# Expert weights' low parts on VectorE, and a float64 decode that checks instead of zeroing and starts one expert earlier

## The chip, the cores and the metric

The kernel runs on one core of a Trainium2 chip. The metric is the device time of one execution, in microseconds (us). Engines are named as in the profile: PE (matrix engine, PEld its weight loads), DVE (vector), ACT (scalar), POOL (GpSimd) and SP (the engine that issues nearly all DMAs, in one order). The engines run side by side, each works through its own instructions strictly in order, and they wait for one another by semaphores.

## The reference

Three layers follow one another. The attention is a recurrence over 768 steps for 4 x 8 heads with a 40 x 40 state. Its output, 3072 tokens of 320 numbers, goes to a mixture of 8 experts, each token to the one with the largest logit. A dense layer follows. Cut to the parts in which the change lies:

```python
x = attn_out.transpose(0, 2, 1, 3).reshape(3072, 320)
expert_idx = argmax(x @ w_gate, axis=1)
for e in range(8):                        # w1[e]: 320x1024, w2[e]: 1024x320, float32
    xe = x[expert_idx == e]
    out[expert_idx == e] = gate * (maximum(xe @ w1[e], 0) @ w2[e])
h = out @ w_in                            # 320x2048, given in float64
g = maximum(h, 0) + alpha * minimum(h, 0)
return (g @ w_out).astype(float32)        # 2048x320, given in float64
```

## The kernel before

The program has three stretches: attention with routing, the eight experts (here expert 0 to expert 7), and the dense layer in six blocks of 512 tokens. A scheduler fixes each engine's order at build time; the program text and `issue_after` only bound it. The change lies in the experts' stretch.

**An expert.** Up to 448 tokens of one expert are computed together. Matmuls take float32 operands rounded to a high part, and a second, low part is added by more matmuls. `hidden` makes one slice of 128 hidden units: eight matmuls into `ph`, then ACT writes the high part `hh` (L1048) and DVE the low parts (L1051, once 64 columns of `hh` and once `hl`). `layer2` then multiplies `hh` and `hl` with the second weights into the sums `po`: eleven matmuls. PE takes `hidden` of slice f+1 before `layer2` of slice f, and `ph` has two buffers, so PE stops when `hh` or `hl` of a slice comes too late. Expert 0 is computed in two halves of its tokens.

**Weights of an expert** (`prep_expert`). Seven DMAs bring `w1[e]` and `w2[e]` into a ring of three buffers `raw`. ACT copies each to the high part (L985, L1001), and the engine `eng` subtracts the high part from `raw` (L987, L989, L1002): six subtractions per expert, 128x1024 twice, 64x1024, 128x960 twice, 128x640. Only then is the `raw` buffer free. For expert 0 `eng` is DVE, for experts 1 to 7 POOL. Three places hold split weights, so expert e+3 can be prepared once expert e has ended.

**The decode** (`decode`, `from_f64`). `w_in` and `w_out` are turned from float64 to float32 in 20 pieces of 128x512: SP loads a piece as pairs of 32-bit words (`r64`, two buffers, 512 KB), DVE builds the float32 bits in three operations (L214, L215, L216), ACT squares the upper words (L217, `sq`, one buffer), and a fourth DVE operation (L218) multiplies by "square at least 2^-30 in float terms", so that numbers too small for the bit trick become zero. SP writes the result (`dec`, 256 KB) to DRAM. It begins in the program text at expert 1, slice 0, after that slice's `hh` and `hl`. The dense layer's weights are read back from expert 6 on.

**A flag** collects conditions under which a general, slow version of the kernel has to run (never with these inputs); `to_flag` reduces it over the partitions with a transposition on PE, at expert 1, slice 4.

Of the kernel before, what the change touches and what calls it, by code (L numbers as in the profile page):

```python
# [8 lines left out]
F32 = mybir.dt.float32  # L9
# [3 lines left out]
U32 = mybir.dt.uint32  # L13
AF = mybir.ActivationFunctionType
ALU = mybir.AluOpType
AX = mybir.AxisListType
# [3 lines left out]
P = 128  # L20
B, H, S, D = 4, 8, 768, 40
N = B * S
DM = H * D
E = 8
F1 = 1024
F2 = 2048
# [13 lines left out]
def f32(ap):  # L40
    return ap.bitcast(F32)
# [168 lines left out]
def from_f64(nc, dst, raw, sq):  # L210

    lo, up = raw[..., 0], raw[..., 1]
    t = dst.bitcast(U32)
    nc.vector.tensor_scalar(t, up, 0x07FFFFFF, 3, op0=ALU.bitwise_and, op1=ALU.logical_shift_left)  # L214
    nc.vector.scalar_tensor_tensor(t, up, 0xC0000000, t, op0=ALU.bitwise_and, op1=ALU.bitwise_or)  # L215
    nc.vector.scalar_tensor_tensor(t, lo, 29, t, op0=ALU.logical_shift_right, op1=ALU.bitwise_or)  # L216
    nc.scalar.activation(sq, f32(up), AF.Square)  # L217
    nc.vector.scalar_tensor_tensor(dst, sq, 2.0 ** -30, dst, op0=ALU.is_ge, op1=ALU.mult)  # L218


def words(ap):
# [10 lines left out]
def whole(gen):  # L232
    for _ in gen:
        pass
# [695 lines left out]
class Moe:  # L930
# [27 lines left out]
    def decode(self, src, name):  # L958

        nc = self.nc  # L960
        n = 512
        out = self.dp.tile(list(src.shape), F32, name=name)
        flat = lambda ap: ap.rearrange("r c -> (r c)").rearrange("(p n) -> p n", p=P)
        to, wo = flat(out), words(flat(src))
        for c in range(0, to.shape[1], n):
            r64 = self.r6.tile([P, n, 2], U32, name="r64", bufs=2)
            nc.sync.dma_start(r64, wo[:, c:c + n])
            dec = self.r6.tile([P, n], F32, name="dec", bufs=2)
            sq = self.r6.tile([P, n], F32, name="sq", bufs=1)
            from_f64(nc, dec, r64, sq)  # L970
            nc.sync.dma_start(to[:, c:c + n], dec)
        return out

# [95 lines left out]
    def run(self, ctx, to_flag):  # L1069
        nc, k, tc = self.nc, self.k, self.tc  # L1070
        for i in (1, 2):
            self.wp.append(ctx.enter_context(tc.tile_pool(name=f"fm_w{i}", bufs=1, reuse_waits="tile")))
        cp = ctx.enter_context(tc.tile_pool(name="fm_c", bufs=1, reuse_waits="tile"))
# [5 lines left out]
        sums = lambda: [p.tile([P, DM], F32, name=f"po{t}") for t, p in enumerate((pa, pa, pb, pb))]  # L1079
        r6 = ExitStack()  # L1080
        self.r6 = r6.enter_context(tc.tile_pool(name="fm_r6", bufs=1, reuse_waits="tile"))
        load = self.load_x(0, EARLY)
        nxt = win = prep = w_in = w_out = None
        for e in range(E):
            w1s, w2s = self.wts[e]
            po = sums()
            ye = sp.tile([P, 4, DM], F32, name="ye", tag="orow", bufs=1)
            ys = self.rt.ys_d[e * CAP:(e + 1) * CAP, :]

            def group(xt, t0, t1, x0, tiles, ts=None, between=None):  # L1090

                ts = ts or range(t0, t1)
                n = min(t1 * P, CAP) - t0 * P
                prev = None
                for f in range(NF1):
                    hh, hl = tiles(f)
                    self.hidden(w1s, f, xt, x0, x0 + n, hh, hl)
                    if prev is not None:
                        self.layer2(po, *prev, w2s, f - 1, NF1, True, ts, t0)
                    prev = hh, hl  # L1100
                    if between:
                        between(f)
                self.layer2(po, *prev, w2s, NF1 - 1, NF1, True, ts, t0)

            def to_sbuf(t):
                if t == 3:
                    nc.scalar.copy(ye[:HT, t, :], po[t][HT:])  # L1107
                    nc.vector.tensor_tensor(ye[:HT, t, :], po[t][:HT], ye[:HT, t, :], op=ALU.add)
                else:
                    (nc.vector.tensor_copy if t % 2 else nc.scalar.copy)(ye[:, t, :], po[t])  # L1110

            def between(f):
                nonlocal nxt, win, prep, w_in, w_out
                if e == E - 2 and f == 4:
                    win = self.whole("win")
                    prep = self.prep_in(win, w_in, nc.gpsimd)
                if e == E - 2 and f >= 4:
                    for _ in range(2):
                        next(prep, None)
                if e == E - 1:  # L1120
                    with tc.issue_after(self.hh_i.ins):
                        next(prep, None)
                if f == 1 and e + 1 < E:
                    with tc.issue_after(self.rt.last.ins), tc.issue_after(self.x_dma.ins):
                        whole(self.prep_expert(e + 1, nc.gpsimd))
                if (e, f) == (1, 4):
                    to_flag(self.psum_t(P)[:1])
                if (e, f) == (1, 0):
                    with tc.issue_after(self.hh_i.ins), tc.issue_after(self.hl_i.ins):
                        w_in, w_out = self.decode(self.w_in, "w_in"), self.decode(self.w_out, "w_out")  # L1130
                if f == 4 and e + 1 < E:
                    nxt = self.load_x(e + 1)()

            ring = lambda f: [sp.tile([P, 4 * P], F32R, name=n, tag=n) for n in ("hh", "hl")]
            if e == 0:
                group(self.xt0, 0, EARLY, 0, lambda f: [self.ap.tile([P, EARLY * P], F32R, name=n, bufs=2) for n in ("ehh", "ehl")])
                xt = load()
                group(xt, EARLY, 4, 0, ring, between=between)
            elif e == E - 1:

                hs = [[hp.tile([P, 2 * P], F32R, name=f"{n}{f}") for n in ("hh", "hl")] for f in range(NF1)]
                group(xt, 0, 2, 0, lambda f: hs[f], (0,), between)
                to_sbuf(0)
                nc.sync.dma_start(ys[:P, :], ye[:, 0])
                with tc.issue_after(self.last.ins):
                    for f in range(NF1):
                        self.layer2(po, *hs[f], w2s, f, NF1, True, (1,))
                    group(xt, 2, 4, 2 * P, ring)
            else:
                group(xt, 0, 4, 0, ring, between=between)  # L1150
            for t in range(1 if e == E - 1 else 0, 4):
                to_sbuf(t)
            for rows, to in self.rows(ye, ys, 1 if e == E - 1 else 0):
                nc.sync.dma_start(to, rows)
            if e == E - 2:
                r6.close()
                hp = ctx.enter_context(tc.tile_pool(name="fm_h", bufs=1, reuse_waits="tile"))
                wout = self.whole("wout")
                prep = self.prep_out(wout, w_out, nc.gpsimd)
                win = win.rearrange("p (c f) -> p c f", c=5)  # L1160
                wout = wout.rearrange("p (s f d) -> p s f d", s=2, d=DM)
            xt = nxt
# [5 lines left out]
        for i in range(N // BT):  # L1168
            po = sums()
            prev = None  # L1170
            for f in range(NF2):
                ph = pg.tile([P, BT], F32, name="ph")
                gemm_k(nc, ph, win, f * P, (f + 1) * P, xt, 0, BT)
                g = sp.tile([P, BT], F32, name="g")
                nc.vector.tensor_scalar(g, ph, 0.0, al[:, f:f + 1], op0=ALU.min, op1=ALU.mult)  # L1175
                nc.vector.scalar_tensor_tensor(g, ph, 0.0, g, op0=ALU.max, op1=ALU.add)  # L1176
                hh = sp.tile([P, BT], F32R, name="gh", tag="hh")
                hl = sp.tile([P, BT], F32R, name="gl", tag="hl")
                lo = split(nc, hh, hl, g, nc.gpsimd)
                if prev is not None:  # L1180
                    self.layer2(po, *prev, wout, f - 1, NF2, False)
                prev = (hh, hl)
                if f == 8 and i + 1 < N // BT:
                    with tc.issue_after(lo.ins):
                        nxt = self.load_x2(i + 1, E * CAP)
# [14 lines left out]
def the_kernel(tc, r, kk, v, w, a, b, wP, kbP, aP, rvP, vrow, w_gate, w1, w2, w_in, w_out, alpha, out):  # L1200
    nc = tc.nc
    with ExitStack() as ctx:
# [6 lines left out]
        k.upper = cp.tile([P, P], BF16, name="upper")  # L1209
        k.iota8 = cp.tile([P, E], F32, name="iota8")  # L1210
        okm = cp.tile([P, 1], F32, name="okm")
        flag = cp.tile([1, 3], F32, name="flag")
        flag_i = cp.tile([1, 1], I32, name="flag_i")

        def to_flag(pk):

            nc.tensor.transpose(pk, okm, k.ident)
            nc.vector.tensor_reduce(flag[:, 0:1], pk, axis=AX.X, op=ALU.min)
            nc.vector.tensor_scalar(flag[:, 0:1], flag[:, 0:1], 0.5, None, op0=ALU.is_lt)
            nc.vector.tensor_reduce(flag[:, 2:3], flag[:, 0:2], axis=AX.X, op=ALU.max)  # L1220
            nc.vector.tensor_copy(flag_i, flag[:, 2:3])
# [62 lines left out]
```

## Time and profile before

| | |
|---|---|
| median of 3 runs | 1208.76 us (1205.51, 1208.76, 1222.03) |
| the profiled execution's own time | 1201.46 us |
| its span in the trace | 1199.7 us |
| busy: PE, DVE, ACT, POOL | 89%, 63%, 47%, 46% of the span |
| experts 0 to 7 in the trace | 570.5 to 842 us |
| dense layer | 842 us to the end |

PE is busy for most of the span, but the share is an average over stretches. A waiting engine does not show in it, and neither does PE's clock, which stands beside it as a share of full speed. A row of a group names the line of the kernel, the engine, the operation and "output <- input"; queue rows (SPq) are DMA issues.

### The profile page before, as it was taken

Reading aid. Unit: us, or ns where it says so; the run is one execution under the profiler, and the core shown is the slowest. Engines: PE = TensorE matmul, PEld = TensorE weight load, DVE = VectorE, ACT = ScalarE, POOL = GpSimd, SP = SyncE. Lnnn points to the kernel's source line nnn. Section 1 sums busy time; section 2 is a strip of 40 time slices with the busy share of each in tenths; the row PEclk is TensorE's granted clock in tenths of the full one; section 3 lists DMA queues with packets and bytes.
Section 4 is the critical chain, followed back from the end, with each engine's and each line's share of the span. In section 5 each row is a group of like instructions: output and inputs, shape, how many; then the busy total and the mean of one; then the engine's idle time right before and its main releaser. Section 6 shows DMA issues by size and latency. Waiting matters only on the chain.

```text
span 1199.7 us, 24756 instructions
## 1 busy us (share of the span) xinstructions
PE 1064.8 (89%) x9565; PEld 945.1 (79%) x9565; DVE 758.7 (63%) x1536; ACT 563.9 (47%) x1412; POOL 556.1 (46%) x498
## 2 busy tenths in 40 slices
PE   2659989988979989888897988999999999999997
PEld 2548777767868868776886877999899999999996
DVE  9896596997796987845369787333444444454542
ACT  3543568666666767887454434444121222121211
POOL 6636156467267362522574334445343435343432
PEclk7655689888789889999999898999999999999999
DMA  3531222232223211252687776442000000000100
GB/s 113 144 128 43 47 69 77 62 81 76 50 71 90 63 44 40 67 150 51 194 259 240 242 229 206 135 123 85 15 22 22 23 23 22 23 25 20 38 8 25
DMA packets 98080, 103.35 MB, mean 86 GB/s; under 512 B 58404, under 2 KB 78884, under 8 KB 97956
## 3 DMA queue, kind: packets, MB, share of 16 engines
q1 hardware_dynamic: 95652, 93.83, 27.1%
q0 software_dynamic: 2304, 7.87, 2.1%
q8 instruction: 78, 1.28, 0.4%
q14 instruction: 46, 0.38, 0.1%
HBM read 79.39 MB, written 22.28 MB: 85 GB/s over the span
## 4 chain that ended last, share of the span: by engine, by line
PE 57%; DVE 23%; issue 6%; DMA 5%; ACT 5%; POOL 3%; SPq 0%; DVEq 0%; POOLq 0%; ACTq 0%
PE ph L238 20%; PE po L238 19%; DVE tmp L506 4%; DVE ut L508 3%; PE lp L461 3%; PE pp L572 2%; PE yc L628 2%; PE yp L538 2%; PE zp L532 2%; DVE q L435 2%; PE sa L612 1%; DMA raw<-in_moe_w_dram 1%; DVE sm L632 1%; DVE dec L215 1%; PE rp L600 1%
## 5 line engine op out<-in xcount | busy, mean ns | idle before, releaser
L229 POOL TENSOR_TENSOR gl<-g,gh 128x512 fp32r<-128x512 f32 x96 | 123.9, 1293 | 211.8 <-ACT gh L228 128.1
L228 ACT ACTIVATE gh<-g 128x512 fp32r<-128x512 f32 x96 | 60.7, 632 | 249.4 <-DVE g L1176 173.9
L1175 DVE TENSOR_SCALAR g<-ph,al 128x512 f32<-128x512 f32 x96 | 72.1, 751 | 156.9 <-POOL gl L229 77.0
L238 PE MATMUL ph<-x2thi,win 128*128 128x512 f32 x480 | 157.0, 392 | 0.0
L238 PE MATMUL po<-wout,gh 128*128 128x320 f32 x768 | 139.0, 309 | 0.0
L238 PEld LDWEIGHTS po<-wout,gh 128*128 128x128 f32 x768 | 122.0, 188 | 5.4
L238 PE MATMUL ph<-x2tlo,win 128*128 128x512 f32 x288 | 113.5, 394 | 0.0
L238 PE MATMUL po<-we,hh 128*128 128x320 f32 (+1 forms) x480 | 92.3, 320 | 19.1 <-DVE hh L1051 12.4
L238 PE MATMUL ph<-xthi,we 128*128 128x448 f32 (+2 forms) x360 | 98.6, 346 | 2.7 <-ACT ye L1107 2.6
L238 PEld LDWEIGHTS ph<-x2thi,win 128*128 128x128 f32 x480 | 88.5, 188 | 13.2
L238 PEld LDWEIGHTS po<-we,hh 128*128 128x128 f32 (+1 forms) x480 | 75.6, 185 | 24.6 <-DVE hh L1051 13.8
L506 DVE TENSOR_TENSOR tmp<-ul,ut 128x31 f32<-128x31 f32 (+15 forms) x186 | 90.7, 487 | 3.3
L461 PE MATMUL lp<-kb,abd 128*128 128x128 f32 x352 | 66.2, 343 | 25.9 <-DVE la L469 12.1
L508 DVE TENSOR_TENSOR ut<-ut,tmp 128x31 f32<-128x31 f32 (+15 forms) x186 | 84.3, 453 | 3.6
L586 POOL TENSOR_SCALAR_AFFINE_SELECT va<-vg 64x512 f32<-64x512 f32 x48 | 37.2, 776 | 99.1 <-ACT vg L585 51.7
L238 PE MATMUL po<-wout,gl 128*128 128x320 f32 x384 | 82.9, 311 | 0.0
L461 PEld LDWEIGHTS lp<-kb,abd 128*128 128x128 f32 x352 | 57.5, 245 | 29.6 <-POOL abd L442 14.1
L442 POOL TENSOR_TENSOR abd<-ra,q 40x512 f32<-40x512 f32 x44 | 61.7, 1403 | 37.5 <-PE ap L485 16.8
L238 PE MATMUL ph<-xtlo,we 128*128 128x448 f32 (+2 forms) x216 | 74.7, 346 | 0.0
L238 PEld LDWEIGHTS ph<-xthi,we 128*128 128x128 f32 x360 | 67.0, 196 | 6.7 <-ACT ye L1107 2.9
L1176 DVE SCALAR_TENSOR_TENSOR g<-ph,g 128x512 f32<-128x512 f32 x96 | 66.3, 690 | 3.1
L238 PEld LDWEIGHTS po<-wout,gl 128*128 128x128 f32 x384 | 64.1, 188 | 2.8
(208 smaller groups left out, 2442.7 us busy)
## 6 DMA issues: line engine op xcount, KB each, us to landing
raw<-in_moe_w_dram SPq DMA_DIRECT2D x16, 512.0 KB
rv<-in_rvP_dram SPq DMA_DIRECT2D x48, 160.0 KB
raw<-in_moe_w_dram SPq DMA_DIRECT2D x16, 480.0 KB
kb<-in_kbP_dram SPq DMA_DIRECT2D x44, 160.0 KB
r<-in_moe_w_in_dram SPq DMA_DIRECT2D x10, 512.0 KB
r<-in_moe_w_out_dram SPq DMA_DIRECT2D x10, 512.0 KB
xs_d<-tt SPq DMA_DIRECT2D x8, 560.0 KB
raw<-in_moe_w_dram SPq DMA_DIRECT2D x16, 256.0 KB
```

The source lines that it names most:

```text
L228: nc.scalar.activation(hi, src, AF.Copy)
L229: return lo_eng.tensor_tensor(lo, src, f32(hi), op=ALU.subtract)
L238: return nc.tensor.matmul(out, lhsT=lhsT, rhs=rhs, start=start, stop=stop)
L435: nc.vector.tensor_tensor_scan(qt.rearrange("p a c t -> p (a c t)"), wz[:, :nw], self.d1q, 0.0, ALU.mult, ALU.max)
L442: nc.gpsimd.tensor_tensor(abd[r, :, q * C:(q + 1) * C], ra[r], qc[r, :, :C], op=ALU.mult)
L461: nc.tensor.matmul(lp[:, i], lhsT=abd[:, i, c2, :], rhs=kb[:, i, c2, :], start=True, stop=True)
L506: nc.vector.tensor_tensor(tv, ul[:, j, j + 1:].unsqueeze(2).to_broadcast([P, n, m]), ut[:, j, :m].unsqueeze(1).to_broadcast([P, n, m]), op ...
L508: nc.vector.tensor_tensor(ut[:, j + 1:, :m], ut[:, j + 1:, :m], tv, op=ALU.subtract)
L532: nc.tensor.matmul(zp[lo, c2, u], lhsT=l1[hi, 2 * half + c2, u, :], rhs=tt[hi, c2, u, q * 64 + 32:q * 64 + 64], start=True, stop=True)
L586: nc.gpsimd.affine_select(x.va[:C].rearrange("p a b c -> p (a b) c")[:, :, D:], x.vg[:C].rearrange("p a b c -> p (a b) c")[:, :, D:], patt ...
L1175: nc.vector.tensor_scalar(g, ph, 0.0, al[:, f:f + 1], op0=ALU.min, op1=ALU.mult)
L1176: nc.vector.scalar_tensor_tensor(g, ph, 0.0, g, op0=ALU.max, op1=ALU.add)
```

## The change

1. Experts 1 to 7: the subtractions (L987, L989, L1002) go from POOL to DVE. The dense layer's own weights stay on POOL.
2. The decode uses `from_normal_f64`: three DVE operations as before and no fourth; ACT squares and then runs a second operation, relu(1 - 2^30 x square), whose sum per partition goes into one column of `below`. A column above zero means that there was a number to be zeroed.
3. The decode begins in the program text at expert 0, slice 3 (second half), not at expert 1, slice 0.
4. `to_flag` takes the maximum of `below` into the condition and is called at the dense layer's first block, slice 4.

```diff
+def from_normal_f64(nc, dst, raw, sq, one, below):
+    lo, up = raw[..., 0], raw[..., 1]
+    t = dst.bitcast(U32)
+    nc.vector.tensor_scalar(t, up, 0x07FFFFFF, 3, op0=ALU.bitwise_and, op1=ALU.logical_shift_left)
+    nc.vector.scalar_tensor_tensor(t, up, 0xC0000000, t, op0=ALU.bitwise_and, op1=ALU.bitwise_or)
+    nc.vector.scalar_tensor_tensor(t, lo, 29, t, op0=ALU.logical_shift_right, op1=ALU.bitwise_or)
+    nc.scalar.activation(sq, f32(up), AF.Square)
+    nc.scalar.activation(sq, sq, AF.Relu, bias=one, scale=-2.0 ** 30, accum_out=below)
...
-            from_f64(nc, dec, r64, sq)
+            from_normal_f64(nc, dec, r64, sq, self.one, self.below[:, self.nb:self.nb + 1])
+            self.nb += 1
...
-                        whole(self.prep_expert(e + 1, nc.gpsimd))
-                if (e, f) == (1, 4):
-                    to_flag(self.psum_t(P)[:1])
-                if (e, f) == (1, 0):
+                        whole(self.prep_expert(e + 1, nc.vector))
+                if (e, f) == (0, 3):
                     with tc.issue_after(self.hh_i.ins), tc.issue_after(self.hl_i.ins):
                         w_in, w_out = self.decode(self.w_in, "w_in"), self.decode(self.w_out, "w_out")
...
+                if (i, f) == (0, 4):
+                    to_flag(self.psum_t(P)[:1], self.below)
...
-        def to_flag(pk):
+        def to_flag(pk, below):
+            nc.vector.tensor_reduce(low, below, axis=AX.X, op=ALU.max)
+            nc.vector.scalar_tensor_tensor(okm, low, 0.0, okm, op0=ALU.is_le, op1=ALU.mult)
```

In the changed kernel the numbers of these lines are higher: L214, L215, L216 are L225, L226, L227; L987, L989, L1002 are L999, L1001, L1014; L1051 is L1063; L967 and L971 (load and write of a piece) are L978 and L983.

DVE where expert 1 ends and expert 2 goes on: `ye` are the copies of expert 1's output, `hh` and `hl` after them belong to expert 2. Before:

```order
L1110 COPY ye<-po_7716 128x320
L1108 TENSOR_TENSOR ye<-po_7718,ye 64x320
L218 SCALAR_TENSOR_TENSOR dec<-sq,dec 128x512
L214 TENSOR_SCALAR dec<-r_7795 128x512
L215 SCALAR_TENSOR_TENSOR dec<-r_7795,dec 128x512
L216 SCALAR_TENSOR_TENSOR dec<-r_7795,dec 128x512
L1051 SCALAR_TENSOR_TENSOR hh<-ph,hh 128x64
L1051 SCALAR_TENSOR_TENSOR hl<-ph,hh 128x384
```

The same place now (`we_8497` are the weights of expert 4):

```order
L1126 COPY ye<-po_7922 128x320
L1124 TENSOR_TENSOR ye<-po_7924,ye 64x320
L227 SCALAR_TENSOR_TENSOR dec<-r_7694,dec 128x512
L999 TENSOR_TENSOR we_8497<-raw,we_8497 128x1024
L225 TENSOR_SCALAR dec<-r_7705 128x512
L999 TENSOR_TENSOR we_8497<-raw,we_8497 128x1024
L226 SCALAR_TENSOR_TENSOR dec<-r_7705,dec 128x512
L1001 TENSOR_TENSOR we_8497<-raw,we_8497 64x1024
L1063 SCALAR_TENSOR_TENSOR hh<-ph,hh 128x64
L1063 SCALAR_TENSOR_TENSOR hl<-ph,hh 128x384
```

Four decode operations stood between the outputs of expert 1 and the next `hh`; now three of the decode and three subtractions stand there. Over the experts the 20 pieces stand at 4, 5, 7 and 4 writes in experts 0, 1, 2 and 3; before they stood in experts 1 to 4.

POOL after the last routed row (the scatter into `xs_d`), before:

```order
L901 DMA xs_d<-xr,sli 3584x320 x2
L987 TENSOR_TENSOR we_7535<-raw,we_7535 128x1024 x2
L989 TENSOR_TENSOR we_7535<-raw,we_7535 64x1024
L1002 TENSOR_TENSOR we_7535<-raw,we_7535 128x960 x2
L1002 TENSOR_TENSOR we_7535<-raw,we_7535 128x640
```

And now:

```order
L912 DMA xs_d<-xr,sli 3584x320 x2
L1096 MEMSET one 128x1
L999 TENSOR_TENSOR win<-raw,win 128x1024 x2
L1001 TENSOR_TENSOR win<-raw,win 64x1024
L999 TENSOR_TENSOR win<-raw,win 128x1024 x2
```

From the end of the routing to the dense layer's weights (`win`, expert 6) POOL has no tile left to work on.

SP in expert 2, between the writes of expert 1's and expert 2's outputs, now (each written piece is followed by a load; the rows left out are the weights of expert 4):

```order
L983 DMA w_out<-dec 128x512
L978 DMA r_7745<-in_moe_w_out_dram 128x1024
L983 DMA w_out<-dec 128x512
L978 DMA r_7755<-in_moe_w_out_dram 128x1024
L983 DMA w_out<-dec 128x512
L978 DMA r_7765<-in_moe_w_out_dram 128x1024
L1027 DMA xe<-xs_d 128x3x320
L1027 DMA xe<-xs_d 64x320
L983 DMA w_out<-dec 128x512
L978 DMA r_7775<-in_moe_w_out_dram 128x1024
```

Seven pieces are loaded and seven written in this stretch, beside seven DMAs of weights; in the kernel before five were loaded and six written between these two outputs.

## Rows read from the trace of the kernel before

**Rows 1.** Stretches (experts 0-5): PE, PEld, DVE, ACT, POOL busy; clock; DMA share, GB/s.

```profile
570.50:613.00 42.50, 38.27 (x264) 35.25 (x265) 15.66 (x56) 21.88 (x43) 25.61 (x13) 0.94 0.67 203
613.00:646.50 33.50, 29.43 (x164) 26.35 (x163) 29.02 (x42) 15.93 (x27) 19.00 (x8) 0.97 0.83 261
646.50:684.80 38.30, 31.73 (x171) 28.83 (x169) 31.97 (x47) 16.23 (x28) 14.38 (x6) 0.91 0.84 259
684.80:722.40 37.60, 32.41 (x164) 28.89 (x164) 30.81 (x48) 16.40 (x28) 14.22 (x6) 0.91 0.69 221
722.40:756.20 33.80, 28.61 (x155) 26.00 (x156) 22.47 (x34) 13.85 (x24) 14.17 (x6) 0.90 0.54 162
756.20:784.10 27.90, 27.90 (x166) 26.02 (x165) 8.77 (x23) 12.66 (x22) 13.20 (x6) 1.00 0.48 144
```

**Rows 2.** Waits, 569 to 735: total us, times, longest.

```profile
ACT sq L217 <- DVE dec L218: 24.5, 8, 6.0
PE po L238 <- DVE hh L1051: 12.4, 5, 4.4
ACT we L985 <- DMA raw<-in_moe_w_dram: 11.8, 9, 3.5
ACT sq L217 <- DMA r<-in_moe_w_out_dram: 9.7, 3, 5.2
DVE dec L214 <- DMA w_out<-dec: 6.2, 3, 3.5
PE po L238 <- ACT hh L1048: 5.0, 3, 1.7
```

**Rows 3.** Instructions in time, after expert 1's end: start, us; brackets: idle before, releaser.

```profile
649.82 1.87 DVE L218 SCALAR_TENSOR_TENSOR dec<-sq,dec 128x512 f32<-128x512 f32 x1
...
650.75 0.52 ACT L1048 ACTIVATE hh<-ph 128x448 fp32r<-128x448 f32 x1
...
653.08 1.29 PE L238 MATMUL po<-we,hh 128*128 128x320 f32 x7
654.00 2.41 POOL L989 TENSOR_TENSOR we<-raw,we 64x1024 fp32r<-64x1024 f32 x1
654.24 2.72 DVE L215 SCALAR_TENSOR_TENSOR dec<-r,dec 128x512 uint32<-128x512 uint32 x1
...
657.60 0.21 DVE L1051 SCALAR_TENSOR_TENSOR hh<-ph,hh 128x64 fp32r<-128x64 f32 x1
...
657.87 0.90 PE L238 MATMUL po<-we,hh 128*128 128x320 f32 x2 [3.50 <-DVE hh L1051]
```

**Rows 4.** The decode's operations on tile dec: ns min/median/max.

```profile
L214 DVE TENSOR_SCALAR dec<-r x20: 409/423/2596, 612.1 to 735.2; 128x512 uint32<-128x512 uint32 x20
L215 DVE SCALAR_TENSOR_TENSOR dec<-r,dec x20: 676/693/2833, 614.5 to 735.7; 128x512 uint32<-128x512 uint32 x20
```

**Rows 5.** Decode's DVE instructions alone, sum over experts 0 to 6.

```profile
sum 238.80, DVE 85.00; mean DVE 12.14
```

**Rows 6.** Subtractions of weights by engine (tile raw): ns min/median/max.

```profile
L987 POOL TENSOR_TENSOR we<-raw,we x14: 2367/2404/3959, 583.0 to 760.8; 128x1024 fp32r<-128x1024 f32 x14
...
L1002 DVE TENSOR_TENSOR we<-raw,we x3: 815/1158/1159, 538.1 to 543.8; 128x960 fp32r<-128x960 f32 x2, 128x640 fp32r<-128x640 f32 x1
L987 DVE TENSOR_TENSOR we<-raw,we x2: 1224/1256/1289, 530.5 to 533.7; 128x1024 fp32r<-128x1024 f32 x2
```

**Rows 7.** The chain that ended last, one step of expert 4: start, us.

```profile
738.16 1.61 PE po L238 x11
```

**Rows 8.** Groups on ACT: count | busy us, mean ns | idle before, releaser.

```profile
L402 ACT ACTIVATE q<-wz,mid 104x512 f32<-104x512 f32 x20 | 14.4, 719 | 10.7 <-DMA wz<-in_wP_dram 10.3 <-POOL yt L648 0.2
...
L217 ACT ACTIVATE sq<-r 128x512 f32<-128x512 f32 x20 | 13.5, 673 | 51.5 <-DVE dec L218 24.5 <-issue 14.3 <-DMA r<-in_moe_w_out_dram 9.7
...
L402 ACT ACTIVATION_READ_ACCUMULATOR q<-wz,mid 104x1 f32 x20 | 3.8, 188 | 0.0
```

**Rows 9.** Stretches, the fullest 5 us of expert 2; columns as before.

```profile
650.00:655.00 5.00, 3.45 (x23) 2.58 (x21) 4.96 (x3) 2.39 (x4) 4.92 (x3) 1.00 1.05 357
```

More of the change, by code (lines that the diff above doesn't have):

```diff
@@ L1081, in run @@
         self.r6 = r6.enter_context(tc.tile_pool(name="fm_r6", bufs=1, reuse_waits="tile"))
+        self.below = cp.tile([P, 2 * DM * F2 // (P * 512)], F32, name="below")
+        self.one = cp.tile([P, 1], F32, name="one")
+        nc.gpsimd.memset(self.one, 1.0)
+        self.nb = 0
         load = self.load_x(0, EARLY)
@@ L1211, in the_kernel @@
         okm = cp.tile([P, 1], F32, name="okm")
+        low = cp.tile([P, 1], F32, name="low")
         flag = cp.tile([1, 3], F32, name="flag")
         flag_i = cp.tile([1, 1], I32, name="flag_i")
-        def to_flag(pk):
+        def to_flag(pk, below):
+            nc.vector.tensor_reduce(low, below, axis=AX.X, op=ALU.max)
+            nc.vector.scalar_tensor_tensor(okm, low, 0.0, okm, op0=ALU.is_le, op1=ALU.mult)
             nc.tensor.transpose(pk, okm, k.ident)
```

## The prediction

> **What bounds the kernel now.** I read the page's share of busy time first and left it: it averages over stretches. The view by stretches [rows 1] shows where PE is not the bound. Expert 5 takes 27.9 us, PE is busy for 27.90 of them at full clock: that is the floor of an expert. Experts 1 to 4 take 33.5, 38.3, 37.6 and 33.8, together 143.2 against 4 x 27.9 = 111.6. So 31.6 us are lost beside the decode. PE's busy times there add up to 122.2, so 21.0 are idle time and 10.6 a clock below full (0.91 and 0.90), half a microsecond of clock for each idle one.
>
> The view of waits [rows 2] names the cause: PE waits 12.4 us for DVE's `hh` and 5.0 for ACT's. The instructions in time [rows 3] show one case. PE works on `hh` of other columns from 653.08, then stands still for 3.50 us until DVE writes `hh` at 657.60. Ahead of it in DVE's order are four decode operations from 649.82 on, and one of them takes 2.72 us while a subtraction of 2.41 runs on POOL. The same operation takes 0.69 at the median and 2.83 at most, L214 0.42 and 2.60 [rows 4]. So DVE's decode operations, whose operands all lie in SBUF, are held up by POOL's subtractions. Over all pieces the decode costs DVE 85.0 us [rows 5]; unhindered, 20 x (0.42 + 3 x 0.69) = 50. The other 35 are this hindrance.
>
> **The change, part by part.** *Subtractions.* DVE takes 1.256 us for 128x1024, 1.16 for 128x960 and 0.815 for 128x640, POOL 2.404 for the first [rows 6]. With 64x1024 priced like 128x1024 (the same length per partition) an expert costs DVE 3 x 1.256 + 2 x 1.158 + 0.815 = 6.9 us, seven experts 48.
>
> *Decode.* Three operations without POOL beside them cost 0.42 + 2 x 0.69 = 1.81 us a piece, 36 for 20, against 85.0. DVE's total thus stays: -85 + 36 + 48 = -1. What changes is the place and the length of a single block. Expert 5's DVE work without decode is 8.77 [rows 1]. With it, experts 1 to 4 need about 24.7 (5 pieces), 28.3 (7), 22.9 (4) and 15.7 us; expert 0 needs 15.66 + 2 x 6.9 + 4 x 1.81 = 36.7 of its 42.5. The total stays but experts 1 to 4 carry 92 instead of 114.
>
> *A single block.* A slice takes PE 1.61 for `layer2` [rows 7] and, with `hidden` and the transpositions, 27.9 / 8 = 3.5. Less ACT's 0.52 and DVE's 0.21 for `hh` [rows 3] and the hand-overs, DVE may be some 2.4 us late without PE noticing. An operation of 2.7 does not fit in that, one subtraction and a decode operation (1.95) do.
>
> *Where an expert ends*, three decode operations and three subtractions now stand ahead of `hh`: 0.69 + 1.26 + 0.42 + 1.26 + 0.69 + 1.26 = 5.6 us. Put at 649.82 they would give `hh` at 655.4, where PE came to need it at 657.87 - 3.50 = 654.37. So a wait of about 1.0 stays of 3.50.
>
> *ACT.* The second operation is not in the trace. The nearest row is a square with an accumulated sum, 0.72, and the read of the sum, 0.19 [rows 8]: 0.91 a piece, 18 us in all. In expert 2 ACT has 12.66 [rows 1] + 7 x (0.67 + 0.91) = 23.7 of 27.9, so it fits beside PE, and 0.91 fits in the slack of a slice. Its two-sided bound is 0 (hidden) and 20 x 0.91 = 18 if nothing hid it; I take 0. Against it, `sq` no longer waits for DVE, which held ACT's queue for 24.5 us [rows 2].
>
> *The flag* moves; its instructions work on one column or one row. I take nothing; exposed, five of them at the 0.21 of a 64-column `hh` would be about 1 us (an estimate), and SP, which loads the flag, has only output writes behind it there.
>
> *DMA.* A piece moves 768 KB, 0.79 MB. Expert 2 without decode moves what expert 5 does, 144 GB/s x 27.9 us = 4.0 MB [rows 1]; with 7 pieces 9.5 MB. At expert 2's present 259 GB/s for a share of 0.84, a full share gives 308, so 9.5 MB need 30.9 us: 3.0 above the floor. It is the one expert in which both DVE (28.3) and DMA exceed PE. Experts 1 and 3 need less (8.0 and 7.2 MB). The burst of 357 GB/s [rows 9] shows that more is possible for 5 us. The Trainium skill (DMA: Bandwidth & Descriptors, Where 436 GB/s comes from) gives about 358 GB/s as a core's limit from HBM; by it 9.5 MB would take 26.6 us, the 3.0 would fall away and the time would be 1183. The burst agrees with that page, expert 2's whole stretch does not reach it, so I keep 3.0.
>
> *Expert 0* gets four pieces and 3.1 MB more, which lifts its 203 GB/s to 277. For it speaks that each `raw` buffer is free 1.15 us earlier (2.40 - 1.26); twelve transfers go through three buffers, at most 4 x 1.15 = 4.6, and 42.5 - 38.27 = 4.2 are idle. Bounds: -7 (all its idle time and slow clock) and +6 (each piece costs 1.5); I take -2, nearer to the four rounds than to the end.
>
> **Sum.** Of the 31.6, what stays: 3.0 in expert 2; three ends of experts at 1.0, with half for clock 4.5; half of PE's 5.0 for ACT, behind late weights, 2.5, with clock 3.8. Together 11.3, so 20.3 are gained, with expert 0's 2 some 22. The profiled execution took 1201.5, which gives 1179; it lies 7.3 below the median of the three runs, 1208.8, against which I forecast **1186**.
>
> **Rivals.** *All to the floor.* The queues clear: experts 1 to 4 at 27.9 gain 31.6, expert 0 up to 7. Against the median: 1170 to 1177. For it: expert 5 shows no wait at all with POOL's subtractions beside it, and DVE has spare time in all but expert 2. Against: the DMA share would have to exceed 0.9 in experts 0 to 2. The DMA limit of the Trainium skill's page named above would allow it. 0.22.
>
> *The subtractions bring their waits along.* POOL waited for ACT's copies at no cost. Now `hh` is queued behind a subtraction whose `raw` is late. ACT waited 11.8 us for first-layer weights [rows 2]; if DVE passes all of it on to PE, with half for clock, 17.7 of the 22 go: 1204, and between 1197 and 1204 if most goes. Against: ACT's own `hh` stands behind the same copies already, so much of that wait is paid today. 0.19.
>
> *Slower: late pieces stop DVE.* L214 waits for its piece; before, such waits were 6.2 us in three cases on DVE and 9.7 in three on ACT (3.2 each) [rows 2]. Now subtractions and `hh` stand behind them on one engine, and after one subtraction only 2.4 - 1.26 = 1.1 of slack is left. Were all 20 pieces 3.2 late, 20 x 2.1 = 42 would be idle, with clock 63, in place of 31.6: 1219 to 1240, about 1230. It turns slower once pieces are on average 1.1 + 31.6 / 1.5 / 20 = 2.2 us late. For it: the share near 1.0 in expert 2. Against: a piece comes every 27.9 / 7 = 4.0 us and two are loaded ahead. 0.06.
>
> That the change doesn't do what it says is excluded by the orders shown: POOL has no expert weights left. My forecast, 1177 to 1197, keeps 0.53.
>
> **Range and chances.** 1169 to 1204 takes in the floor, the forecast and most of the third case. Two per cent, about what a measurement of this kernel can tell from no change, are 24 us, a time below 1184.6. The floor (0.22) and two fifths of the forecast (0.21) are below: faster 0.43. Slower by 24 us is 0.04, within 0.53.
>
> **What would show it.** DVE's decode operations at 0.42 and 0.69 throughout; experts 1, 3 and 4 within 2 us of 27.9 and expert 2 at 30 to 32 with a DMA share over 0.9; no wait of ACT's squares for DVE. I am wrong if experts 1 to 3 stay above 33 us, if PE's waits for `hh` go on with a DMA named behind them, or if expert 0 grows past 48.

## The result, and the profile after

The changed kernel takes 1196.26 us (median of 20 runs) where the kernel before takes 1209.51 in the same session: ratio 0.9885, 95% interval 0.9859 to 0.9911, so about 13 us faster where 22 were forecast. Both kernels, whatever the edit, have executions some per cent longer than their others; ratios and intervals leave these out, and of the profiles below only that of moved_only is of such a one. The profiled run of after took 1194.1 us, its span 1192.4, against 1201.5 and 1199.7 before: 7.3 us less. (The profiled run of before lies 8 us below its median, that of after 2.) By stretches, each expert from the ACT copy of the last tile (64 rows) of the one ahead to its own, expert 0 from PE's first matmul into its `ph`, and the dense stage from the last such copy to the end:

| us | expert 0 | 1 | 2 | 3 | 4 | 5 to 7 | dense stage |
|---|---|---|---|---|---|---|---|
| before | 42.3 | 33.5 | 38.3 | 37.6 | 33.8 | 85.9 | 357.7 |
| after | 50.0 | 33.7 | 31.8 | 29.1 | 27.9 | 85.6 | 361.5 |

(The stage ahead of expert 0, which the change leaves alone, ended 2.1 us later in this profile.) Experts 1 to 4 went from 143.2 to 122.5, 20.7 less where 20.3 were forecast. Expert 0 grew by 7.7 and the dense stage by 3.8; these two and the 2.1 are what separates 20.7 from the 7.3 of the whole. The view by stretches, experts 0 to 4; columns as in [rows 1]:

```profile
572.76:622.76 50.00, 42.47 (x261) 37.76 (x259) 32.45 (x74) 27.10 (x54) 2.07 (x3) 0.88 0.77 232
622.76:656.46 33.70, 31.17 (x164) 28.55 (x163) 24.34 (x46) 20.08 (x37) 0.00 (x0) 0.88 0.82 267
656.46:688.26 31.80, 29.77 (x172) 27.05 (x172) 24.82 (x47) 21.38 (x41) 0.00 (x0) 1.00 0.91 295
688.26:717.36 29.10, 27.29 (x157) 24.27 (x156) 22.05 (x44) 18.10 (x34) 0.00 (x0) 1.00 0.76 244
717.36:745.26 27.90, 27.90 (x166) 25.98 (x166) 15.23 (x29) 12.68 (x21) 0.00 (x0) 1.00 0.48 146
```

Experts 2 to 4 now have the full clock, and POOL (fifth busy time) is out of all of them. Experts 0 and 1 have 0.88 where [rows 1] has 0.94 and 0.97. DVE's operations that read tile `r`, ns min/median/max, which answer to [rows 4]:

```profile
L225 DVE TENSOR_SCALAR dec<-r x20: 410/420/429, 604.8 to 706.8; 128x512 uint32<-128x512 uint32 x20
L226 DVE SCALAR_TENSOR_TENSOR dec<-r,dec x20: 678/685/696, 605.8 to 707.2; 128x512 uint32<-128x512 uint32 x20
L227 DVE SCALAR_TENSOR_TENSOR dec<-r,dec x20: 673/686/694, 610.7 to 708.4; 128x512 uint32<-128x512 uint32 x20
```

The longest is 0.70 us where it was 2.83: nothing holds them up any more. Their sum is 20 x (0.420 + 0.685 + 0.686) = 35.8 us for the 85.0 of [rows 5]. PE's waits from 570 to 745 (total us, times, longest), which answer to [rows 2]:

```profile
PE tr_ps L276 <- DMA xe<-xs_d: 5.6, 3, 2.5
PE po L249 <- DVE hh L1063: 3.4, 2, 1.8
...
PE po L249 <- ACT hh L1060: 2.1, 1, 2.1
```

and before, the line on `xe` that [rows 2] leaves out:

```profile
PE tr_ps L265 <- DMA xe<-xs_d: 2.0, 3, 0.9
```

The waits for DVE's `hh` fell from 12.4 us to 3.4 and those for ACT's from 5.0 to one of 2.1. The waits for `xe`, the next expert's rows, grew from 2.0 to 5.6. The three longest besides DVE's (2.53 and 2.33 for `xe`, 2.11 for ACT) are in experts 0 and 1. What each does to the clock, in stretches of 4 us of experts 0 and 1 (the last three numbers are clock, DMA share and GB/s):

```profile
604.00:608.00 4.00, 1.67 (x9) 1.08 (x8) 3.09 (x9) 1.52 (x4) 0.00 (x0) 0.89 1.02 230
608.00:612.00 4.00, 4.00 (x17) 3.84 (x18) 2.56 (x4) 3.66 (x6) 0.00 (x0) 0.50 0.47 134
612.00:616.00 4.00, 4.00 (x27) 3.98 (x26) 3.58 (x7) 1.19 (x3) 0.00 (x0) 0.76 0.83 268
616.00:620.00 4.00, 1.89 (x11) 1.43 (x10) 2.49 (x5) 2.64 (x7) 0.00 (x0) 1.00 1.03 408
620.00:624.00 4.00, 4.00 (x15) 3.29 (x16) 3.95 (x10) 3.91 (x9) 0.00 (x0) 0.59 1.06 224
```

PE stood still for 2.33 us in the first of them and 2.11 in the fourth. Behind each the granted clock is at or near 0.50, the lower of its two levels (1.2 GHz). So expert 0's PE is idle for 50.00 - 42.47 = 7.5 us in place of 4.2, and busy for 42.5 in place of 38.1 (the stretch of [rows 1] begins a little earlier) with the same work: of the 7.7, some 3.3 are waiting and 4.4 clock.

How the second of these waits came about stands in the chain of work that ended last (start, us, what):

```profile
601.53 6.71 DMA raw<-in_moe_w_dram
...
608.32 1.07 ACT we L997
609.41 1.23 DVE we L1001
610.66 0.70 DVE dec L227
611.38 0.34 SPq L983
...
611.77 5.47 DMA r<-in_moe_w_in_dram
...
617.33 0.69 ACT sq L228
```

This is read from the top. Expert 1's weights landed late (6.71 us); a subtraction waited for them; the last operation of a piece's decode stood behind that subtraction on DVE; its write to DRAM (L983) waited on SP; the load of the next piece stood behind the write on SP; ACT waited for that piece. And on ACT, `hh` stood behind it, as ACT's instructions in time show:

```profile
617.33 0.69 ACT L228 ACTIVATE sq<-r 128x512 f32<-128x512 f32 x1 [2.59 <-DMA r<-in_moe_w_in_dram]
618.04 0.72 ACT L229 ACTIVATE sq<-sq,one 128x512 f32<-128x512 f32 x1
...
619.62 0.33 ACT L1060 ACTIVATE hh<-ph 128x192 fp32r<-128x192 f32 x1
```

PE had done its last matmul ahead of this `hh` at 617.9 and went on at 620.00.

### The profile page after: what moved, and what is told of

It reads as the page before. It is cut to its first block, busy times and chain, and to the rows that moved or that the text cites. A ratio compares the mean times of both kernels' runs of the same rounds, so it can differ in the third digit from the quotient of the medians.

```text
span 1192.4 us, 24778 instructions
## 1 busy us (share of the span) xinstructions
PE 1064.2 (89%) x9565; PEld 940.9 (79%) x9565; DVE 751.7 (63%) x1560; ACT 581.4 (49%) x1452; POOL 456.0 (38%) x457
## 3 DMA queue, kind: packets, MB, share of 16 engines
q8 instruction: 78, 1.28, 0.4%
## 4 chain that ended last, share of the span: by engine, by line
PE 61%; DVE 19%; DMA 6%; ACT 5%; issue 5%; POOL 2%; SPq 1%; DVEq 0%; ACTq 0%; POOLq 0%
PE ph L249 21%; PE po L249 20%; DVE tmp L517 4%; DVE ut L519 3%; PE lp L472 3%; PE pp L583 3%; PE yc L639 2%; DMA raw<-in_moe_w_dram 2%; DMA r<-in_moe_w_out_dram 2%; PE yp L549 2%; PE zp L543 2%; PE sa L623 2%; DVE q L446 2%; PE rvp L594 2%; PE rp L611 1%
## 5 line engine op out<-in xcount | busy, mean ns | idle before, releaser
L999 POOL TENSOR_TENSOR win<-raw,win 128x1024 fp32r<-128x1024 f32 x4 | 9.6, 2410 | 198.5 <-ACT win L997 198.4
L597 POOL TENSOR_SCALAR_AFFINE_SELECT va<-vg 64x512 f32<-64x512 f32 x48 | 35.8, 746 | 100.7 <-ACT vg L596 50.9
```

The source lines that it names most:

```text
L597: nc.gpsimd.affine_select(x.va[:C].rearrange("p a b c -> p (a b) c")[:, :, D:], x.vg[:C].rearrange("p a b c -> p (a b) c")[:, :, D:], patt ...
```

## The experiments

The theories. **1**: POOL's subtractions, which hold up DVE, were the cost, as the prediction has it; what is left over is transfers of the early pieces in experts 0 and 1. **2**: the gain comes from the check, since ACT no longer stands behind a square that waits for DVE. **3**: expert 0 grew because DVE subtracts in it. All runs in one table, stretches from one profile each; "4th" is the engine of the decode's last operation. A few us between two profiles are not read: `after` and `aligned` differ by the width of one tile, and by 2.8 us in experts 1 to 4.

| | subtracts | 4th | start in expert | ratio (95%) | expert 0 | 1 to 4 | dense |
|---|---|---|---|---|---|---|---|
| before | POOL | DVE | 1 | 1 | 42.3 | 143.2 | 357.7 |
| subs_only | DVE | DVE | 1 | 0.9887 (0.9808-0.9966) | 44.7 | 131.9 | 357.3 |
| check_only | POOL | ACT | 1 | 0.9940 (0.9901-0.9979) | 43.4 | 130.4 | 361.8 |
| start_undone | DVE | ACT | 1 | 0.9874 (0.9820-0.9927) | 44.0 | 122.2 | 361.2 |
| decode_only | POOL | ACT | 0 | 0.9853 (0.9787-0.9920) | 46.1 | 120.4 | 361.8 |
| after | DVE | ACT | 0 | 0.9885 (0.9859-0.9911) | 50.0 | 122.5 | 361.5 |
| two_loads | DVE | ACT | 0 | 0.9905 (0.9870-0.9941) | 50.3 | 118.5 | 359.8 |
| sq_two | POOL | DVE | 1 | 0.9972 (0.9938-1.0006) | 42.9 | 135.2 | 359.7 |
| flag_early | POOL | ACT | 0 | 0.9881 (0.9816-0.9946) | 45.7 | 120.7 | 362.3 |
| moved_only | POOL | DVE | 1 | 0.9999 (0.9965-1.0034) | | | |
| aligned | DVE | ACT | 0 | 0.9870 (0.9822-0.9919) | 49.4 | 119.7 | 361.8 |
| aligned_pool | POOL | ACT | 0 | 0.9878 (0.9821-0.9935) | 45.6 | 120.8 | 362.1 |
| aligned_late | DVE | ACT | 1 | 0.9883 (0.9842-0.9924) | 45.6 | 121.5 | 361.7 |
| aligned_xpool | DVE | ACT | 0 | 0.9804 (0.9757-0.9852) | 44.4 | 117.1 | 359.8 |

**subs_only**, the kernel before with the subtractions on DVE:

```
-                        whole(self.prep_expert(e + 1, nc.gpsimd))
+                        whole(self.prep_expert(e + 1, nc.vector))
```

> The kernel before with the subtractions of experts 1 to 7 on DVE, and nothing else changed. Theory 1 (POOL's subtractions held up DVE's decode; what the changed kernel still loses comes from decode DMAs in experts 0 and 1): the decode's DVE operations go to 0.42 and 0.69 us in every case, expert 0 stays at 42 to 45 us, experts 1 to 4 together take 125 to 135 instead of 143, the time is 0.985 to 0.993 of before. Theory 2 (the gain is ACT no longer waiting for DVE's fourth decode operation): experts 1 to 4 stay at 140 to 146, ratio 0.997 to 1.003. Theory 3 (expert 0 grew because DVE now subtracts there): expert 0 takes 48 to 51, as in the changed kernel.

Measured 0.9887, experts 1 to 4 at 131.9: 11.3 of the 20.7 us. The decode's operations are at 0.69 at most here too, but PE still waits for `hh`. DVE ahead of one such `hh` of expert 2, in time:

```profile
658.95 2.34 DVE L987 TENSOR_TENSOR we<-raw,we 128x1024 fp32r<-128x1024 f32 x2
661.32 1.22 DVE L989 TENSOR_TENSOR we<-raw,we 64x1024 fp32r<-64x1024 f32 x1
662.58 0.43 DVE L214 TENSOR_SCALAR dec<-r 128x512 uint32<-128x512 uint32 x1
662.92 0.68 DVE L218 SCALAR_TENSOR_TENSOR dec<-sq,dec 128x512 f32<-128x512 f32 x1
663.52 0.21 DVE L1051 SCALAR_TENSOR_TENSOR hh<-ph,hh 128x64 fp32r<-128x64 f32 x1
```

4.6 us of whole-speed work stand in a row ahead of `hh`, and PE waited 2.88 for it at 663.79. So a row can be long enough without POOL's hindrance, which was one way to make it long.

**decode_only**, the change with POOL's subtractions (the line above with its signs turned round, in the changed kernel):

> The changed kernel with the subtractions back on POOL: the new decode and its early start alone. Theory 1: single decode operations on DVE still last up to 2.7 us, experts 1 to 3 take over 33 each, ratio 0.995 to 1.006. Theory 2: experts 1 to 3 take under 33, ratio 0.983 to 0.992. Theory 3: expert 0 is back at 42 to 45; by theory 1 it stays at 48 or more.

Measured 0.9853: theory 1's number is missed, and the kernel is no slower than the whole change. The hindrance is still there, by the rows of tile `dec`:

```profile
L225 DVE TENSOR_SCALAR dec<-r x20: 406/540/2580, 597.0 to 703.7; 128x512 uint32<-128x512 uint32 x20
L226 DVE SCALAR_TENSOR_TENSOR dec<-r,dec x20: 674/692/2755, 598.1 to 704.6; 128x512 uint32<-128x512 uint32 x20
```

They take up to 2.76 us with POOL subtracting, and 0.70 at most in the whole change. By the Trainium skill (SBUF — State Buffer, SBUF: two separate sides) GpSimd operations and VectorE operations in a two-port mode or with two SBUF inputs lock each other out of a shared pair of ports for a whole instruction; these two rows agree. Yet experts 1 to 4 are at 120.4, so with one operation less a piece and some pieces done in expert 0 what is held up is no longer what PE waits for: it waits there for `xtlo` and `hl` instead, 7.5 us idle in all.

**start_undone**, the change with the decode begun in expert 1:

```
-                if (e, f) == (0, 3):
+                if (e, f) == (1, 0):
```

> The changed kernel with the decode begun at expert 1, slice 0, as before. Theory 1: expert 0 is back at 42 to 45 us and experts 1 to 4 share out the 20 pieces at 28 to 33 each; ratio to before 0.982 to 0.989, at least as good as the changed kernel's 0.9885. Theory 3: expert 0 stays at 48 to 51 and the ratio is 0.987 to 0.993.

0.9874; expert 0 is back at 44.0 and experts 1 to 4 are at 122.2 as after the change. Where DVE subtracts, the early start gave experts 1 to 4 nothing and cost expert 0 its 6 us; in `aligned` and `aligned_late` (below), the same pair again, expert 0 takes 49.4 and 45.6, which is 4. In the times the two cannot be told apart.

**two_loads**, the change with only 2 of the 20 pieces loaded and each decoded ten times, so the decode's output is not the weights':

```
-            r64 = self.r6.tile([P, n, 2], U32, name="r64", bufs=2)
-            nc.sync.dma_start(r64, wo[:, c:c + n])
+            if self.nb < 2:
+                r64 = self.r6.tile([P, n, 2], U32, name=f"r64{self.nb}", bufs=1)
+                nc.sync.dma_start(r64, wo[:, c:c + n])
+                ...
+            r64 = self.kept[self.nb % 2]
```

> The changed kernel with only the first two of the decode's 20 loads (all later pieces are decoded from those two, so the dense layer's weights are not the given ones); all decode operations and writes stay. Theory 1: expert 0 takes 42 to 45 us, experts 1 to 3 28 to 30 each, ratio to before 0.970 to 0.980. Theory 3 (DVE's queue, not DMA): expert 0 stays at 48 or more, expert 1 over 32, ratio 0.985 to 0.992.

0.9905, and expert 0 stays at 50.3: theory 1's account of expert 0 falls. PE there waits 1.97, 1.28 and 1.23 us for `hh` of ACT and DVE in place of `xe` and a late piece. With the loads gone the pieces' operations come sooner and stand ahead of `hh` on both engines. So it is the early pieces as work on ACT and DVE, beside the subtractions (theory 3), and not the transfers of their loads alone. Neither alone makes up the 50: expert 0 takes 46.1 us with the early pieces but POOL's subtractions, and 44.0 with DVE's subtractions but no early pieces.

**sq_two** and **check_only** tell theories 1 and 2 apart. The first is the kernel before with

```
-            sq = self.r6.tile([P, n], F32, name="sq", bufs=1)
+            sq = self.r6.tile([P, n], F32, name="sq", bufs=2)
```

> The kernel before with one edit: two buffers in turn for ACT's squares (`sq`) where there was one, so a square need not wait until DVE has read the square of the piece ahead. POOL's subtractions, the four operations of DVE and the start stay. Theory 1 (POOL's subtractions hold up DVE, and PE waits for DVE): the decode operations stay at up to 2.8 us and PE goes on waiting about 12 us for DVE's `hh`; ratio 0.997 to 1.003, experts 1 to 4 together 140 to 145 us. Theory 2 (what cost was ACT standing behind a square that waits for DVE): ACT's 24.5 us of such waits mostly go, and the ratio is 0.985 to 0.993, experts 1 to 4 together 125 to 133 us.

ACT's waits for DVE's last operation are gone from its view of waits, PE still waits 14.3 us for DVE's `hh`, and the ratio is 0.9972 (0.9938 to 1.0006): as theory 1 has it. Experts 1 to 4 came out at 135.2 in its one profile, between both theories' numbers. By the times that wait of ACT was a small part of the gain; the 8.0 us of the profile say more, and nothing here settles between them. The second is start_undone with POOL's subtractions:

> The change with POOL's subtractions and with the decode beginning in expert 1 as before: only the check on ACT in place of DVE's fourth operation, and the later flag, are left of it. Theory 1 (POOL's subtractions): DVE's three remaining operations are still held up; 20 x 0.69 to 2.8 us of DVE's work go, so at most half of the gain: ratio 0.993 to 1.000. Theory 2 (ACT no longer waits for DVE): ratio 0.983 to 0.990, as with the early start, and experts 1 to 4 together below 130 us. If the early start was what helped there, the ratio is 0.995 to 1.000 and experts 1 to 4 stay above 135 us.

0.9940, experts 1 to 4 at 130.4: half the gain, as theory 1 has it, and theory 2's number is missed. Here the waits for DVE's `hh` are 7.0 us.

**flag_early** and **moved_only** ask for the dense stage's 3.8 us. The first is decode_only with the flag made in expert 5:

```
-                if (i, f) == (0, 4):
-                    to_flag(self.psum_t(P)[:1], self.below)
...
+                if (e, f) == (5, 4):
+                    to_flag(self.psum_t(P)[:1], self.below)
```

> The change with POOL's subtractions and with the flag made in the middle of expert 5 in place of the dense stage; the three small tiles (`below`, `one`, `low`) stay where the change puts them. It asks why the dense stage (from the last expert's last copy to the end) takes 361.5 us after the change and 357.7 before. If the flag's instructions in the dense stage cost it: dense stage 357 to 358 us, and the time about 4 us below that of the same kernel with the late flag (1188.0): ratio 0.982. If it is where the later tiles lie in SBUF: dense stage 361 to 362 us, ratio 0.985.

The dense stage stays at 362.3: it is not the flag. The second is the kernel before with the three small tiles laid out and used by nothing:

```
+        below = cp.tile([P, 2 * DM * F2 // (P * 512)], F32, name="below")
+        one = cp.tile([P, 1], F32, name="one")
...
+        low = cp.tile([P, 1], F32, name="low")
```

> The kernel before with the three small tiles of the change (`below`, `one`, `low`) laid out and set to a constant once, used by nothing: later tiles lie where they lie after the change, the rest is as before. If the place of the tiles in SBUF costs the dense stage: 361 to 362 us for it, ratio 1.003. If it is the flag: 357 to 358 us, ratio 1.000.

Its profiled run took 1237.18 us where its median is 1206.70, so its stretches aren't read; its dense matmuls, from 860 to 1100 at a granted clock of 1.00 as in the other two, can be. Groups of the same stretch (xcount | busy us, mean ns), before:

```profile
L238 PE MATMUL ph<-x2thi,win 128*128 128x512 f32 x325 | 106.4, 392 | 0.0
...
L238 PE MATMUL ph<-x2tlo,win 128*128 128x512 f32 x196 | 77.3, 394 | 0.0
```

with the small tiles laid out (moved_only):

```profile
L238 PE MATMUL ph<-x2thi,win 128*128 128x512 f32 x310 | 102.6, 396 | 0.0
...
L238 PE MATMUL ph<-x2tlo,win 128*128 128x512 f32 x186 | 73.7, 396 | 0.0
```

and after the change:

```profile
L249 PE MATMUL ph<-x2thi,win 128*128 128x512 f32 x327 | 108.2, 396 | 0.0
...
L249 PE MATMUL ph<-x2tlo,win 128*128 128x512 f32 x197 | 78.0, 396 | 0.0
```

The 4 and 2 ns are there with nothing but three unused tiles added, which push the later tiles up by 160 B a partition (`win` by 32). check_only and flag_early, with the tiles in the same places, have 396 and 396 too, subs_only and sq_two, without them, 392 and 394. The dense stage as a whole, before and after (PE's busy time stands behind the length):

```profile
842.06:1199.70 357.64, 349.99 (x1973) 317.14 (x1971) 157.47 (x225) 78.62 (x130) 143.97 (x116) 0.99 0.07 22
830.90:1192.40 361.50, 352.13 (x1971) 316.55 (x1969) 157.18 (x225) 78.46 (x129) 143.84 (x116) 0.99 0.07 22
```

PE is busy for 2.1 us more: that much of the 3.8 goes with the places. The other 1.7 are idle time of PE, and all of it lies behind its last matmul, where the last output is written (7.65 us before, 9.37 after). It does not go with the change: sq_two, whose dense matmuls are the old ones, has 9.7 there, and aligned_xpool (below), whose tiles are moved, 7.3. In the time of the whole, 0.9999, an effect of 0.003 is within the interval.

**aligned** is the change with `low` 128 B wide, which pushes the tiles by 256 B (`win` by 128); **aligned_pool** and **aligned_late** are decode_only and start_undone with the same edit:

```
-        low = cp.tile([P, 1], F32, name="low")
+        low = cp.tile([P, 32], F32, name="low")[:, :1]
```

> The change with one edit: the tile `low` is laid out 128 B wide in place of 4 (one column of it is used), so that the tiles of the experts and the dense stage begin 256 B behind their place in the kernel before, a multiple of 64 B, and not 160 B. If the place of the tiles is what costs the dense stage: the dense matmuls (128x512) take 392 to 394 ns again in place of 396, the dense stage 357 to 358 us in place of 361.5, and the ratio is 0.985. If something else of the change costs it: 396 ns, 361 to 362 us, ratio 0.9885.

> The change with `low` 128 B wide and POOL's subtractions: the early start, the check on ACT, and the old place of the subtractions. Theory of places in SBUF: dense stage 357 to 358 us, experts 0 to 4 together as without the wider tile (166.5), so 4 us below 1188: 1184, ratio 0.982. If the dense stage stays at 361.8, ratio 0.985.

> The change with `low` 128 B wide and with the decode beginning in expert 1 as before: DVE subtracts, ACT checks. Theory of places: dense stage 357 to 358 us, experts 0 to 4 as without the wider tile (166.1), expert 0 at 44: 4 us below 1189.8, so 1186, ratio 0.984. If the early start gives anything where DVE subtracts, this kernel is slower than the one with it and the wider tile.

All three missed: dense stages of 361.7 to 362.1, matmuls at 395 and 398 ns in each, ratios of 0.987 to 0.988. So the place matters, but a multiple of 64 B doesn't bring the old times back, and the rule of it stays open. They also repeat decode_only and start_undone: with the check, the other two parts can't be told apart in the time.

**aligned_xpool** is `aligned` with the loads of `xe` issued by POOL, which after the change is idle in the experts:

```
-            self.x_dma = self.nc.sync.dma_start(to, rows)
+            self.x_dma = self.nc.gpsimd.dma_start(to, rows)
```

> The change with `low` 128 B wide and with the loads of the next expert's rows (`xe`) issued by POOL, which has nothing else to do there, in place of SP, where pieces and weights of the decode stand ahead of them. It asks whether expert 0's 50.0 us come from late rows. If so: PE's waits of 2.33 and 2.53 us for `xe` in experts 0 and 1 go, and with them the half clock that follows; experts 0 and 1 together 76 to 78 us in place of 83.7, ratio 0.978 to 0.980. If the transfers share the engines whatever queue they come from, `xe` lands 6 us or more behind its issue as now and the ratio is that of the kernel with the wider tile alone, 0.985. If POOL's issue holds up DVE or comes later, slower: 0.99.

0.9804 (0.9757 to 0.9852), 1182.96 us: faster than the kernel before and, its interval lying wholly below, than the change. Beside `aligned`, the kernel that it edits (0.9870, 1190.50 us), its interval overlaps a little. Experts 0 and 1 take 76.6 us as the first case has it, in place of 83.7 (and of 79.5 in `aligned`). But its mechanism holds only in part. PE's waits from 570 to 745 in `aligned`:

```profile
PE po L249 <- ACT hh L1060: 4.6, 2, 3.7
PE po L249 <- DVE hh L1063: 4.4, 3, 1.7
PE tr_ps L276 <- DMA xe<-xs_d: 3.5, 3, 1.7
```

and in `aligned_xpool`:

```profile
PE tr_ps L276 <- DMA xe<-xs_d: 4.2, 3, 2.6
...
PE po L249 <- DVE hh L1063: 0.6, 1, 0.6
...
PE po L249 <- ACT hh L1060: 0.4, 1, 0.4
```

The wait for `xe` did not go (one of 2.64 us is left in expert 1, 7.7 behind its issue); the waits for `hh` went, from 9.0 us to 1.0. What the edit takes off SP are the waits ahead of those loads: the rows must have been scattered into `xs_d`, and the buffer must have been read by PE. SP stood for both in `aligned`; now POOL does, where nothing but the next such load is queued behind it:

```profile
SPq L1027 <- DMA xs_d<-xr,sli: 9.9, 1, 9.9
SPq L1027 <- PE tr_ps L276: 7.4, 3, 6.2
```

```profile
POOL xe L1027 <- PE tr_ps L276: 142.0, 7, 29.6
```

(SP from 570 to 690 in `aligned`, POOL from 570 to 745 in `aligned_xpool`.) In expert 0, where 5.0 us are gained, lie only 1.2 of the 7.4; the 9.9 end in it, at 585.09. The weights queued behind that first load, on SP in `aligned`, where expert 0 begins at 579.34:

```profile
586.01 2.29 SPq L996 DMA_DIRECT2D raw<-in_moe_w_dram  x4
```

and in `aligned_xpool`, where it begins at 580.64:

```profile
572.59 6.70 SPq L996 DMA_DIRECT2D raw<-in_moe_w_dram  x4
```

So the first four loads of weights are issued some 10 to 15 us sooner, ahead of expert 0 and not in it. That this, and the 6.2 us later on, are why the waits for `hh` went is how I read it; a run that takes only those waits off SP was not made. Of the 6.4 us between the two profiles, 1.9 are the time behind the last matmul.

## Why the prediction was right, and where it was off

**Experts 1 to 4**: 20.7 us for 20.3. The mechanism came as forecast, DVE's row before `hh` got shorter; that the two numbers meet so closely is in part luck. Of the 31.6 us above the floor 10.9 stayed, where the sum had 11.3, but not in the parts priced: 5.8 are in expert 1, a wait of 2.53 for `xe` and the lower clock behind it, for which the sum has no term; the 3.8 for ACT's `hh` did not come, since PE waits for it in none of these four. Of the three ends of experts with a wait of 1.0, two are there with 1.75 and 1.69, at full clock, and one is gone. In time, DVE at the end of expert 1's tail shows the row that the prediction added up, with two waits of its own in it:

```profile
659.38 1.23 DVE L999 TENSOR_TENSOR we<-raw,we 128x1024 fp32r<-128x1024 f32 x1 [0.33 <-ACT we L997]
661.75 0.43 DVE L225 TENSOR_SCALAR dec<-r 128x512 uint32<-128x512 uint32 x1 [1.15 <-DMA r<-in_moe_w_out_dram]
662.10 1.22 DVE L999 TENSOR_TENSOR we<-raw,we 128x1024 fp32r<-128x1024 f32 x1
663.23 0.68 DVE L226 SCALAR_TENSOR_TENSOR dec<-r,dec 128x512 uint32<-128x512 uint32 x1
663.95 1.22 DVE L1001 TENSOR_TENSOR we<-raw,we 64x1024 fp32r<-64x1024 f32 x1
665.20 0.23 DVE L1063 SCALAR_TENSOR_TENSOR hh<-ph,hh 128x64 fp32r<-128x64 f32 x1
```

The rivals of waiting subtractions (0.33) and late pieces (1.15) are both real here, and small. Expert 1 alone broke the sign given for it: 33.7 against "within 2 us of 27.9".

**The cause given for it** was too narrow. The hindrance by POOL is shown (0.70 us at most without it, 2.76 with), but it was named as the whole cause. Each part alone takes 11 to 13 us off experts 1 to 4 (131.9, 130.4), the two pairs that hold the check take 21 and 23 (122.2, 120.4; the third pair was not run), all three no more (122.5). What they share, as I read the traces, is that they shorten the row of DVE's work ahead of `hh`; no run varies that length alone.

**DVE's total and ACT**: 35.8 us of decode for the 36 forecast, and no square waits for DVE. The second operation of ACT, taken at nothing, showed itself once, in expert 0, behind a late piece.

**DMA in expert 2**: 31.8 us at a share of 0.91 is as forecast, but PE waits for no transfer in it; its 2.0 idle us are `hh` (1.75) and `xtlo` (0.3). DVE, forecast at 28.3 us there, was busy for 24.8. The term was right in size for another reason. The limit of 358 GB/s that the prediction took from a page of the Trainium skill is none here: 4 us of expert 0 moved 408. The Trainium skill (HBM Reference, Specifications (TRN2)) says that a core alone gets well above its share, about 425 GB/s, which agrees.

**Expert 0** is the step that failed: -2 was taken between -7 and +6, and it is +7.7, past the 48 us named as proof of error; the 2.11 for ACT's `hh` behind a late piece is also the other sign named, a wait for `hh` with a DMA behind it. The working priced the early pieces as transfers and let the subtractions free buffers sooner. It did not follow the ring of queues in the chain above (subtraction, decode, write and load on SP, ACT), and two_loads shows that without the loads the same work on ACT and DVE costs as much. Its bound of +6 took the pieces alone; by decode_only they cost 3.8 of it alone (46.1), and the rest comes with DVE's subtractions beside them.

**The flag at nothing** held for its instructions (flag_early), but its tiles moved others, and the dense stage's term, 0, measured +3.8: 2.1 of longer matmuls, and 1.7 behind the last one that come and go from profile to profile. With both terms put right the sum is -20.3 + 7.7 + 3.8 = -8.8 beside a measured -7.3 in the profiles; the medians, over 20 runs each, give -13. That is 10 us short of the forecast, within its range, and under the 24 us (two per cent) that the prediction set as the line to "faster".

## What to carry to other kernels

When work is moved ahead in time, follow each of its instructions through the queue it joins, writes and loads on the DMA queue too: one late transfer can go round all engines before it stops TensorE. Several remedies for one wait don't add up, so try each alone; here either of two pairs did all of it, and the third part cost expert 0 four to six microseconds. An engine that a change leaves idle is worth trying for DMA issues that have to wait, for a buffer or for rows: on a busy queue everything behind them waits too.

## What the runs showed of the hardware

The duration of a 128x512 fp32r matmul depended on where tiles lie in SBUF: 392 and 394 ns at the old places, 396 and 396 with later tiles 160 B up, 395 and 398 with 256 B, same order of instructions, full clock, and nothing else changed in moved_only. Which tile and which distance count was not found.
